# Infini-attention block: attention results kept channels-by-tokens, regrouped by DMAs, with the memory read-out transposed instead

## The chip, the cores and the metric

The kernel is one program on one core of a Trainium2 chip. The metric is the device time of one execution in microseconds (us). The core has five engines that run side by side, each working through its own queue in order: TensorE (PE, matmuls and transposes; its weight loads are listed as PEld), VectorE (DVE), ScalarE (ACT), GpSimd (POOL) and SyncE (SP), which issues nearly all DMAs of this kernel. A DMA is issued in order by its queue, moves on 16 shared DMA engines, and has landed some microseconds later.

## The reference

A transformer block over 2048 tokens of 512 channels (32 heads of 16), with the tokens in four segments of 512. The attention half, per segment `s`:

```python
logits = jnp.einsum("bhqd,bhkd->bhqk", qs, ks) * scale + mask
p = _softmax(logits, axis=-1)
a_dot = jnp.einsum("bhqk,bhkd->bhqd", p, vs)
pq = phi(qs)
num = jnp.einsum("bhld,bhde->bhle", pq, M)
den = jnp.einsum("bhld,bhd->bhl", pq, z)[..., None] + 1e-6
a_mem = num / den
o = g * a_mem + (1.0 - g) * a_dot
...
M = M + jnp.einsum("bhld,bhle->bhde", pk, vs)
z = z + jnp.einsum("bhld->bhd", pk)
```

The `o` of all heads is multiplied by `wo`, scaled and added to the input; a layer norm and a bilinear gated feed-forward layer follow. Everything is float32; large products are made from two-part splits (a high part `H` and a remainder `L`).

## The kernel before, in words

**Units.** The 32 heads stand in four groups (`g`) of eight; a group's channels fill 128 partitions. A unit `u` is four heads of one segment: `u = 8 s + 2 g + j`, 32 units in all, two to each segment and group (`ug = u // 2`).

**The loop** (lines 998 to 1039) runs over `v` from -2 to 32 with five slots each, and its order is written out by hand: PE's instructions are chained one behind the other (`pe`, line 73), DVE's too (`Chain`); those of ACT, POOL and SP are ordered by the framework's planner. In slot `i` of turn `v` come score products for a later unit (`q_step`, PE, then a masked row maximum on DVE), the products that are exponentiated for unit `v` (`k_step`, PE, ACT `pt`, then a causal select on POOL), and in slot 1 the products with the values for unit `v-1` (`av_step`, 32 matmuls into `tb`). `av_step` leaves in `tsb` (ACT, line 353), for each of the four heads `j`, 16 rows of numerators at partition `32 j` and one row of row sums at `32 j + 16`, each row 512 tokens long.

Before a unit's `k_step` its row maxima go through DVE (`n_split`), a PE transpose (`ntp`), a DVE copy `nt` and two 4 KB DMAs into `qst` (`n_step`, line 304, emitted in slot 2 of the turn before). In slot 1 stand the two 384 KB loads of a unit three turns ahead (line 259), which read what the projections wrote (`kd`, `qd`, lines 715 and 718).

**`t_step`** (lines 355 to 380, slot 4) turns `tsb` to tokens-by-channels: four PE transposes into `tr`, a DVE reciprocal of the row sums, a DVE multiplication into `orow`. For the second unit of a group POOL adds the memory part (`memb`, loaded in line 364, for `s > 0`) and SP writes 256 KB to `od` (line 379).

**Filler.** Projections, memory, and after them the output projection are generators (`fill_a`, `fill_b`) whose steps `fill` (line 929) puts between the slots. Four of the five slots add 0.25 x 5.5 = 1.375 credits; a step takes its yielded credits off, and filling goes on while credit is positive. A yielded `False` ends the filling of that slot whatever the credit.

**Memory** (`a_mem`, line 768): for `s > 0` it reads the running memory with `phi(q)` (`up`), divides (DVE `den`, POOL `mem`, lines 792 to 794) and writes 256 KB to `memd` (line 795).

**Output projection**: `wo_load` brings `od` back, `wo_op` (line 425) transposes it again, 128 x 128 blocks, four for each group, into a PSUM bank `op`, and splits that into `oH` (ACT) and `oL` (DVE); `wo_row` multiplies by `wo`; `wo_mm` runs 4 x 4 such rows. `osegs` counts the segments whose `od` is complete.

After the loop the feed-forward layer runs on PE: `product` (line 1100), woven with the preparation of weights (`prep`, line 384), then `acc`.

## Time and profile before

| what | us |
|---|---|
| median of 3 runs | 889.91 |
| lowest and highest run | 889.39, 892.38 |
| the profiled execution | 892.53 |
| its span, first to last instruction | 890.8 |
| PE busy / DVE busy | 848.3 / 660.8 |
| ACT busy / POOL busy | 471.0 / 417.9 |

The profile is of one execution. Its span is the time between the first and the last instruction; 1.7 us of the execution lie around it. Busy time is a union over an engine's instructions. The ends of matmuls are modelled, and neighbouring matmuls overlap, so the start-to-start distance of two of them says more of PE's pace than their durations do. Rows of the queue of SP show how long it took to issue a DMA, and "landing" is the time from issue until the data was there.

### The profile page before, as it was taken

To read this page: it belongs to the slowest core of one execution; us is meant where nothing else is said; L and a number is where in the kernel's file an instruction comes from. 1 tells how busy PE (TensorE), PEld (TensorE's weight loads), DVE (VectorE), ACT (ScalarE), POOL (GpSimd) and SP (SyncE) were. 2 spreads that over 40 slices of the span, in tenths; PEclk is the share of its full clock that TensorE was granted. 3 is DMA by queue.
4 is the path that set the end of the run, shared out by engine and by line. 5 is a ranking of instruction groups with operands and counts; after the bars stand their busy time and mean duration, and the time that the engine had idled before them with its cause. 6 is when DMAs were issued, how large, how long until landed. Compare 5 with 4: busy or idle time off the path is not lost.

```text
span 890.8 us, 14534 instructions
## 1 busy us (share of the span) xinstructions
PE 848.3 (95%) x4951; PEld 598.1 (67%) x4952; DVE 660.8 (74%) x1756; ACT 471.0 (53%) x730; POOL 417.9 (47%) x564
## 2 busy tenths in 40 slices
PE   8988999999999999999899898999999999999998
PEld 5755666665665556565556466878878888887886
DVE  8588877897788987678788649798884856666532
ACT  3756867777677775577444654333262622333321
POOL 4544545566546574466623423887500746560000
PEclk9998999999999999999899999999999999999999
DMA  7673543746446543657861453444402341222032
GB/s 237 216 229 114 185 122 104 240 155 199 139 125 201 163 140 123 184 164 225 257 214 61 131 164 105 144 143 123 167 26 97 93 140 48 71 54 92 0 116 95
DMA packets 103515, 124.85 MB, mean 140 GB/s; under 512 B 11984, under 2 KB 71376, under 8 KB 103440
## 3 DMA queue, kind: packets, MB, share of 16 engines
q1 hardware_dynamic: 103296, 123.90, 45.3%
q8 instruction: 39, 0.64, 0.3%
q14 instruction: 36, 0.29, 0.1%
q10 hardware_dynamic: 144, 0.02, 0.0%
HBM read 80.17 MB, written 43.45 MB: 139 GB/s over the span
## 4 chain that ended last, share of the span: by engine, by line
PE 65%; DVE 16%; DMA 8%; ACT 5%; POOL 3%; issue 2%; SPq 1%; DVEq 0%; POOLq 0%; ACTq 0%
PE g L86 20%; PE acc L86 14%; PE tb L86 6%; DVE q L40 6%; PE k L86 5%; PE q L86 5%; PE vps L86 4%; PE kps L86 2%; PE qps L86 2%; PE wops L86 2%; ACT pt L324 2%; DMA qd<-q 2%; DMA qst<-qd 1%; PE up L86 1%; DVE nm L40 1%
## 5 line engine op out<-in xcount | busy, mean ns | idle before, releaser
L40 DVE CUSTOM_DVE_ANT_0 q<-q,cmask 128x384 f32<-128x384 f32 (+3 forms) x512 | 246.7, 508 | 57.9 <-PE q L86 47.8
L324 ACT ACTIVATE pt<-k 128x1024 f32<-128x1024 f32 x160 | 163.8, 1024 | 76.5 <-PE k L86 74.2
L327 POOL TENSOR_SCALAR_AFFINE_SELECT pt<-pt 128x256 f32<-128x256 f32 (+1 forms) x224 | 99.0, 455 | 175.4 <-ACT pt L324 172.0
L86 PE MATMUL q<-kst,qst 96*128 96x384 bf16 (+3 forms) x512 | 102.4, 303 | 9.2 <-DVE nm L40 6.5
L86 PE MATMUL k<-qst,kst 98*128 98x384 bf16 (+3 forms) x512 | 98.4, 305 | 8.0 <-ACT pt L324 6.3
L400 POOL TENSOR_TENSOR w<-w 128x256 f32<-128x256 f32 (+1 forms) x84 | 72.4, 872 | 60.4 <-DMA w<-in_w_up_dram 57.8
L397 POOL TENSOR_TENSOR AL<-w,AH 128x512 fp32r<-128x512 f32 (+1 forms) x42 | 59.3, 1412 | 55.4 <-ACT AH L396 54.4
L86 PE MATMUL tb<-pt,v 128*32 128x512 f32 (+3 forms) x1024 | 76.3, 438 | 0.9 <-POOL pt L327 0.9
L86 PEld LDWEIGHTS <-kst 98*128 98x128 bf16 x512 | 39.0, 99 | 50.9 <-issue 42.8
L40 DVE DVE_READ_ACCUMULATOR2_ANT nm<- 128x1 f32 x512 | 72.0, 141 | 0.0
L396 ACT ACTIVATE AH<-w 128x512 fp32r<-128x512 f32 (+2 forms) x88 | 47.3, 565 | 45.7 <-POOL w L400 22.4
L86 PEld LDWEIGHTS <-qst 96*128 96x128 bf16 x512 | 43.8, 98 | 36.2 <-issue 10.0
L1319 DVE TENSOR_TENSOR mL<-mid,mH 128x512 fp32r<-128x512 f32 (+1 forms) x44 | 32.2, 735 | 41.5 <-ACT mH L1318 40.5
L86 PE MATMUL acc<-DH,mH 128*128 128x512 f32 x144 | 57.2, 397 | 0.0
L86 PE MATMUL acc<-DH,mL 128*128 128x512 f32 x144 | 56.6, 393 | 0.2 <-DVE mL L1319 0.2
L86 PE MATMUL acc<-DL,mH 128*128 128x512 f32 x144 | 56.5, 393 | 0.0
L86 PEld LDWEIGHTS tb<-pt,v 128*32 128x32 f32 x1024 | 28.7, 110 | 40.4 <-issue 34.7
L1318 ACT ACTIVATE mH<-mid 128x512 fp32r<-128x512 f32 (+1 forms) x44 | 27.1, 626 | 51.2 <-PE acc L86 50.2
L1114 ACT ACTIVATE p<-g 128x512 f32<-128x512 f32 (+1 forms) x22 | 13.1, 597 | 69.2 <-PE g L86 69.2
L397 DVE TENSOR_TENSOR AL<-w,AH 128x512 fp32r<-128x512 f32 (+3 forms) x44 | 33.8, 772 | 18.5 <-ACT AH L396 18.5
L353 ACT ACTIVATE tsb<-tb 128x512 f32<-128x512 f32 x32 | 19.1, 596 | 38.7 <-PE tb L86 38.6
L86 PE MATMUL g<-t_0H,AH 128*128 128x512 f32 (+1 forms) x88 | 34.6, 394 | 1.1 <-DVE u L1123 1.0
(278 smaller groups left out, 2097.9 us busy)
## 6 DMA issues: line engine op xcount, KB each, us to landing
kst<-kd SPq DMA_DIRECT2D x32, 384.0 KB, 4.3
qst<-qd SPq DMA_DIRECT2D x32, 384.0 KB, 5.1
wm<-in_w_mod_dram SPq DMA_DIRECT2D x24, 256.0 KB, 5.2
kd<-k SPq DMA_DIRECT2D x16, 384.0 KB, 3.8
qd<-q SPq DMA_DIRECT2D x16, 384.0 KB, 3.2
w<-in_w_gate_dram SPq DMA_DIRECT2D x40, 128.0 KB, 2.5
w<-in_w_up_dram SPq DMA_DIRECT2D x40, 128.0 KB, 3.1
wd<-dwd SPq DMA_DIRECT2D x6, 768.0 KB, 4.6
```

The lines of the kernel that those rows point to most:

```text
L40: i = getattr(self.eng, name)(*a, **k)
L86: return pe(nc.tensor.matmul(*a, **k))
L324: lpt[0] = act.activation(pt, kp, AF.Exp, scale=0.25)
L327: sels[u, i] = nc.gpsimd.affine_select(w, w, pattern=[[0, w.shape[1]], [1, P]], compare_op=ALU.is_ge, fill=0.0, base=0, channel_multiplier=-1)
L353: act.activation(tsbs[u], tbs.pop(u), AF.Copy)
L396: pin(act.activation(hi[sl], w[sl], AF.Copy))
L397: eng.tensor_sub(lo[sl], w[sl], hi[sl].bitcast(F32))
L400: pin(ce.tensor_tensor(w[:, o, :, 0:n], w[:, x, :, 0:n], w[:, y, :, 0:n], op=op))
L1114: act.activation(r["p1"], ps, AF.Copy)
L1318: pin(act.activation(mH[0:n], md[0:n], AF.Copy))
L1319: vec.tensor_sub(mL[0:n], md[0:n], mH[0:n].bitcast(F32))
```

## The change: what it does

- `od`, `orow`, `memb` and `memd` become channels-by-tokens, 128 partitions (channels of a group) by 512 tokens.
- `t_step` moves from slot 4 to slot 2 and issues eight DMAs instead of transposing: four spread a row of 512 row sums over 64 partitions x 8 (`rds`, 2 KB each), four copy 16 numerator rows to their place in `orow` (32 KB each). `r_step` (slot 4 of even turns) takes one DVE reciprocal for both units of a group and writes it to DRAM (`rdd`, 16 KB); `rb_step` (slot 1 of the next turn) reads it back with each row repeated for 16 partitions (256 KB); `o_step` (slot 3) multiplies on POOL, adds the memory part on POOL and writes `od`. The last group keeps the old way.
- `a_mem` transposes the memory read-out (four PE transposes into `mT`, an ACT copy `mTs`) before it writes `memd`, for 11 of the 12 groups with memory.
- `wo_op` no longer transposes, except for the last group: `oH` and, in place, `oL` come straight from the loaded tile. Its steps yield 0 instead of 0.45; for segment 0 `paced` turns each into `False`; those of segments 1 and 2 are woven into `wo_mm` of the segment before.
- The wait for `osegs` moves behind `wo_mm(0)`. After the loop, the first feed-forward block takes its weight preparation in other places. Tile tags and buffer counts follow.

```diff
--- before.py
+++ after.py
@@ -1,5 +1,5 @@
 from contextlib import ExitStack
-from itertools import chain
+from itertools import chain, islice
 
 import concourse.bass as bass
 import concourse.tile as tile
@@ -133,7 +133,8 @@
     qd = [[dram.tile([6, P, L], BF, name=f"qd{s}_{g}") for g in range(NG)] for s in range(NSEG)]
     kd = [[dram.tile([6, P, L], BF, name=f"kd{s}_{g}") for g in range(NG)] for s in range(NSEG)]
     memd = [[dram.tile([P, 4 * HG * DH], F32, name=f"memd{s}_{g}") for g in range(NG)] for s in range(NSEG)]
-    od = [dram.tile([4, P, D], F32, name=f"od{s}") for s in range(NSEG)]
+    od = [dram.tile([NG, P, L], F32, name=f"od{s}") for s in range(NSEG)]
+    rdd = [dram.tile([HG, L], F32, name=f"rdd{ug}") for ug in range(NSEG * NG - 1)]
     x1d = [[dram.tile([P, D], F32, name=f"x1d{s}_{t}") for t in range(4)] for s in range(NSEG)]
 
     def rows(s, t):
@@ -205,7 +206,7 @@
         yield from ln_rows(pool, xt, s, pfx)
         hH, hL = [], []
         for d in range(KT):
-            h = pool.tile([P, L], F32, tag="hf" if kept_h is None else "orl", name=f"{pfx}hf{s}_{d}", bufs=hb[2])
+            h = pool.tile([P, L], F32, tag="hf", name=f"{pfx}hf{s}_{d}", bufs=hb[2])
             ln_col(bank(f"{pfx}tp{s}_{d}"), h, xt, d, sc, sh, A)
             hi = hpool.tile([P, L], F32R, tag=hb[0].format(d), name=f"{pfx}hH{s}_{d}", bufs=hb[1])
             lo = hpool.tile([P, L], F32R, tag=hb[0].format(4 + d), name=f"{pfx}hL{s}_{d}", bufs=hb[1])
@@ -251,7 +252,7 @@
     vec.memset(cmask, 0.0)
     nc.gpsimd.affine_select(cmask, cmask, pattern=[[-1, L]], compare_op=ALU.is_ge,
                             fill=NEG, base=L - P, channel_multiplier=1)
-    orows, mems, ptiles, sels, tbs, tsbs = {}, {}, {}, {}, {}, {}
+    orows, rds, mems, ptiles, sels, tbs, tsbs = {}, {}, {}, {}, {}, {}, {}
 
     def load(u):
         s, g, j = u // 8, u // 2 % 4, u % 2
@@ -352,32 +353,62 @@
             tsbs[u] = ap.tile([P, L], F32, tag="tsb", name=f"tsb{u}", bufs=2)
             act.activation(tsbs[u], tbs.pop(u), AF.Copy)
 
+    def last(ug):
+
+        return ug == NSEG * NG - 1
+
+    def m_load(ug):
+
+        if ug >= NG:
+            mems[ug] = ap.tile([P, L], F32, tag="memb", name=f"memb{ug}", bufs=2)
+            nc.sync.dma_start(mems[ug], memd[ug // NG][ug % NG])
+
     def t_step(u):
 
-        s, g, jq = u // 8, u // 2 % 4, u % 2
-        ug = u // 2
+        jq, ug = u % 2, u // 2
         h0 = jq * HQ
         if jq == 0:
-            orows[ug] = wpool.tile([P, 4, HG, DH], F32, tag="orow", name=f"orow{ug}", bufs=2)
-            if s > 0:
-                mems[ug] = ap.tile([P, 4, HG, DH], F32, tag="memb", name=f"memb{ug}", bufs=2)
-                nc.sync.dma_start(mems[ug].rearrange("p t h e -> p (t h e)"), memd[s][g])
-        orow = orows[ug]
+            orows[ug] = wpool.tile([P, L], F32, tag="orow", name=f"orow{ug}", bufs=2)
         tsb = tsbs.pop(u)
-        tr = pst([P, 4, 4, 32], "sm", f"tr{u}", F32)
-        for t in range(4):
-            TP(tr[:, t].rearrange("p a b -> p (a b)"), tsb[:, t * P:(t + 1) * P], ident)
-        rd = ap.tile([P, 4, 4], F32, tag="rd", name=f"rd{u}", bufs=2)
-        vec.reciprocal(rd, tr[:, :, :, DH])
-        vec.tensor_mul(orow[:, :, h0:h0 + 4, :], tr[:, :, :, 0:DH],
-                             rd.unsqueeze(3).to_broadcast([P, 4, 4, DH]))
+        if last(ug):
+            orow = orows[ug].rearrange("p (t h e) -> p t h e", h=HG, e=DH)
+            tr = pst([P, 4, 4, 32], "sm", f"tr{u}", F32)
+            for t in range(4):
+                TP(tr[:, t].rearrange("p a b -> p (a b)"), tsb[:, t * P:(t + 1) * P], ident)
+            rd = ap.tile([P, 4, 4], F32, tag="rl4", name=f"rl4_{u}", bufs=1)
+            vec.reciprocal(rd, tr[:, :, :, DH])
+            vec.tensor_mul(orow[:, :, h0:h0 + 4, :], tr[:, :, :, 0:DH], rd.unsqueeze(3).to_broadcast([P, 4, 4, DH]))
+            if jq == 1:
+                nc.gpsimd.tensor_add(orows[ug], orows[ug], mems.pop(ug))
+            return
         if jq == 0:
-            return
+            rds[ug] = ap.tile([64, HG, 8], F32, tag="rd", name=f"rd{ug}", bufs=1)
+        for j in range(HQ):
+            nc.sync.dma_start(rds[ug][:, h0 + j], tsb[32 * j + DH:32 * j + DH + 1].rearrange("a (p k) -> a p k", k=8))
+        for j in range(HQ):
+            nc.sync.dma_start(orows[ug][(h0 + j) * DH:(h0 + j + 1) * DH], tsb[32 * j:32 * j + DH])
+
+    def r_step(ug):
+
+        rd = rds.pop(ug)
+        vec.reciprocal(rd, rd)
+        nc.sync.dma_start(rdd[ug].rearrange("h (p k) -> p h k", k=8), rd)
+
+    def rb_step(ug):
+
+        rds[ug] = ap.tile([P, L], F32, tag="rb", name=f"rb{ug}", bufs=1)
+        nc.sync.dma_start(rds[ug], rdd[ug].unsqueeze(1).to_broadcast([HG, DH, L]))
+
+    def o_step(ug):
+
+        s, g = ug // NG, ug % NG
+        o = orows.pop(ug)
+        nc.gpsimd.tensor_mul(o, o, rds.pop(ug))
         if s > 0:
-            nc.gpsimd.tensor_add(orow, orow, mems.pop(ug))
-        if ug < NSEG * NG - 1:
-            nc.sync.dma_start(od[s].rearrange("t p c -> p t c")[:, :, g * P:(g + 1) * P],
-                              orow.rearrange("p t h e -> p t (h e)"))
+            nc.gpsimd.tensor_add(o, o, mems.pop(ug))
+        nc.sync.dma_start(od[s][g], o)
+        if g == NG - 1:
+            osegs[0] += 1
 
     wt = {}
 
@@ -415,30 +446,40 @@
 
     def wo_load(s, pool):
         rw = []
-        for t in range(4):
-            a = pool.tile([P, D], F32, tag="orl", name=f"orl{s}_{t}", bufs=4)
-            n = D - P if s == NSEG - 1 else D
-            pin(nc.sync.dma_start(a[:, 0:n], od[s][t][:, 0:n]))
+        for g in range(NG - 1 if s == NSEG - 1 else NG):
+            a = pool.tile([P, L], F32, tag="orl", name=f"orl{s}_{g}", bufs=4)
+            pin(nc.sync.dma_start(a, od[s][g]))
             rw.append(a)
         return rw
 
     def wo_op(s, pb, rw, us, gs=range(NG)):
 
         for g in gs:
-            op = bank(f"op{s}_{g}")
-            for t in range(4):
-                a = rw[t][:, g * P:(g + 1) * P]
-                if s == NSEG - 1 and g == NG - 1:
-                    a = orows[NSEG * NG - 1][:, t].rearrange("p h e -> p (h e)")
-                TP(op[:, t * P:(t + 1) * P], a, ident)
-            oH = pb.tile([P, L], F32R, tag="oH", name=f"oH{s}_{g}", bufs=6)
-            oL = pb.tile([P, L], F32R, tag="oL", name=f"oL{s}_{g}", bufs=6)
-            act.activation(oH, op, AF.Copy)
+            oH = pb.tile([P, L], F32R, tag="oH", name=f"oH{s}_{g}", bufs=8)
+            if s == NSEG - 1 and g == NG - 1:
+                a = bank(f"op{s}_{g}")
+                for t in range(4):
+                    TP(a[:, t * P:(t + 1) * P], orows[NSEG * NG - 1][:, t * P:(t + 1) * P], ident)
+                oL = pb.tile([P, L], F32R, tag="oH", name=f"oL{s}_{g}", bufs=8)
+            else:
+                a = rw[g]
+                oL = a.bitcast(F32R)
+            act.activation(oH, a, AF.Copy)
             us.append((oH, oL))
-            yield 0.45
-            pin(vec.tensor_sub(oL, op, oH.bitcast(F32)))
-            if g % 2 == 1:
-                yield False
+            yield 0.0
+            pin(vec.tensor_sub(oL, a, oH.bitcast(F32)))
+            yield 0.0
+
+    def both(a, b):
+        while True:
+            x, y = next(a, None), next(b, None)
+            if x is None and y is None:
+                return
+            yield 0.0
+
+    def paced(a):
+        for _ in a:
+            yield False
 
     def xr_load(s, pb):
         xrs = []
@@ -792,7 +833,8 @@
             pin(vec.tensor_scalar_add(den, ups[:, :, :, DH], 1e-6))
             vec.reciprocal(den, den)
             nc.gpsimd.tensor_mul(mem, ups[:, :, :, 0:DH], den.unsqueeze(3).to_broadcast([P, 4, HG, DH]))
-            nc.sync.dma_start(memd[s][g], mem.rearrange("p t h e -> p (t h e)"))
+            if last(s * NG + g):
+                nc.sync.dma_start(memd[s][g], mem.rearrange("p t h e -> p (t h e)"))
         if s < NSEG - 1:
             mz = pst((P, HG, VS), "sm", f"mz{s}_{g}")
             for t in range(4):
@@ -805,6 +847,16 @@
                 vec.tensor_mul(mt, mz, hmg[:, g])
                 nc.gpsimd.tensor_add(MZ[g], MZ[g], mt)
             yield 0.9
+        elif not last(s * NG + g):
+            yield 0.0
+        if s > 0 and not last(s * NG + g):
+            mT = pst((P, L), "sm", f"mT{s}_{g}")
+            for t in range(4):
+                TP(mT[:, t * P:(t + 1) * P], mem[:, t].rearrange("p h e -> p (h e)"), ident)
+            mTs = pa.tile([P, L], F32, tag="mTs", name=f"mTs{s}_{g}", bufs=1)
+            act.activation(mTs, mT, AF.Copy)
+            nc.sync.dma_start(memd[s][g], mTs)
+            yield 0.5
         done.add((s, g, 0))
 
     def a_mod(i, a):
@@ -906,16 +958,15 @@
         pr = prep(0, "0_0", bc, 1, pb, 1)
         next(pr)
         us = [[], [], []]
-        yield from weave(wo_op(0, pb, B["orl"], us[0]), ob, (0, 1, 2, 3))
+        yield from paced(both(wo_op(0, pb, B["orl"], us[0]), ob))
+        yield from weave(wo_mm(0, us[0], pb), both(pr, wo_op(1, pb, o1, us[1])), (1, 3, 4, 6, 7, 9, 10, 12, 13))
         while osegs[0] <= 2:
             yield None
         o2 = wo_load(2, wpool)
-        yield from weave(wo_mm(0, us[0], pb), pr, (3, 6, 9, 12))
-        yield from wo_op(1, pb, o1, us[1])
         lg = lnC(0, pb, bc, pb, "x1", 4)
-        yield from weave(wo_mm(1, us[1], pb), lg, (1, 5, 6, 7, 8, 9, 11, 12, 13, 14))
+        lr = islice(lg, 10)
+        yield from weave(wo_mm(1, us[1], pb), both(lr, wo_op(2, pb, o2, us[2])), (1, 5, 6, 7, 8, 9, 11, 12, 13, 14))
         B["nxt"] = yield from lg
-        yield from wo_op(2, pb, o2, us[2])
         B["orl_free"] = True
         lg = lnC(1, pb, bc, pb, "x1", 4)
         yield from weave(wo_mm(2, us[2], pb), lg, (0, 1, 2, 3, 4, 5, 6, 7, 8, 9))
@@ -1011,7 +1062,7 @@
                     av_step(v - 1, kb)
             if v == NQ and slot == 0:
                 assert B["orl_free"]
-                o3 = wo_load(3, wpool)
+                o3 = wo_load(3, B["pb"])
                 xr3 = xr_load(3, B["pb"])
             if v == NQ and slot == 2:
                 btag[:] = ["ms", "lq0", "ms", "lq1"]
@@ -1023,9 +1074,19 @@
             if prev and slot == 4:
                 if (v - 1) % 2 == 0 and v > 8:
                     until((v - 1) // 8, (v - 1) // 2 % 4, 0)
+                if v % 2 == 1:
+                    m_load((v - 1) // 2)
+                if last((v - 1) // 2):
+                    t_step(v - 1)
+                elif v % 2 == 0:
+                    r_step((v - 2) // 2)
+            if slot == 2 and prev and not last((v - 1) // 2):
                 t_step(v - 1)
-                if (v - 1) % 8 == 7:
-                    osegs[0] += 1
+            if v > 1 and v % 2 == 1:
+                if slot == 1:
+                    rb_step((v - 3) // 2)
+                if slot == 3:
+                    o_step((v - 3) // 2)
             if slot == 2 and prev and (v - 1) % 8 == 7:
                 vfree[0] = (v - 1) // 8 + 2
             fill(share[slot], slot < 4)
@@ -1238,7 +1299,7 @@
             next(sd, None)
             for j in ((5, 6, 3, 7) if q == i == 0 else (6, 5, 2, 7, 3)):
                 product(q, i, j)
-                for _ in range(2 if i == 0 else 1):
+                for _ in range(1 if i else 0 if j == 5 else 3):
                     next(g, None)
                 if 1 < i < 9 and j in (5, 7, 3):
                     next(side, None)
```

## The prediction

> **What bounds the kernel now.** I read the page first, then the stretches of the span, the waits, the groups of instructions and one unit's timeline.
>
> ```profile
> PE 848.3 (95%) x4951; PEld 598.1 (67%) x4952; DVE 660.8 (74%) x1756; ACT 471.0 (53%) x730; POOL 417.9 (47%) x564
> PE 65%; DVE 16%; DMA 8%; ACT 5%; POOL 3%; issue 2%; SPq 1%; DVEq 0%; POOLq 0%; ACTq 0%
> L353 ACT ACTIVATE tsb<-tb x32: 585/597/603, 76.2 to 522.8; 128x512 f32<-128x512 f32 x32
> 100.00:400.00 300.00, 289.91 (x2101) 182.07 (x2100) 243.31 (x866) 210.69 (x308) 168.12 (x251) 1.00 0.53 160
> 424.00:428.00 4.00, 2.31 (x16) 1.58 (x16) 3.14 (x8) 2.45 (x5) 3.78 (x3) 1.00 0.95 295
> 428.00:435.00 7.00, 6.21 (x16) 4.79 (x15) 4.20 (x12) 2.17 (x3) 4.58 (x6) 0.51 1.06 356
> 435.00:531.00 96.00, 88.22 (x629) 54.77 (x628) 67.28 (x214) 50.68 (x68) 31.54 (x62) 0.98 0.45 142
> DVE q L40 <- PE q L86: 31.6, 50, 2.0
> ```
>
> The first row is the page's busy time, the second its chain of work. The third places the loop: 32 units from 76.2 to 522.8 us, so one takes 446.6 / 31 = 14.4 us. The windows give, for each stretch, length, busy time of PE, PEld, DVE, ACT and POOL, granted clock, DMA share and GB/s. Between 100 and 400 us PE is busy 97%, DVE 81%, ACT 70%, POOL 56%; the last row (waits in that window) shows DVE sitting idle for PE for 31.6 us. So PE sets the loop's pace, with DVE close behind, and a saving counts where both become shorter. After 424 us it is looser, with one bad spot (the clock at 0.51), which the change rebuilds.
>
> **The change, part by part: PE.**
>
> ```profile
> L89 PE MATMUL tr<-ident,tsb 128*128 128x128 f32 x128 | 19.8, 277 | 0.1
> L89 PE MATMUL op<-ident,orl 128*128 128x128 f32 x60 | 9.0, 282 | 4.0 <-DVE oL L40 4.0
> L89 PE MATMUL mp<-ident,phk 128*128 128x128 f32 x48 | 7.5, 279 | 0.0
> 339.83 0.60 PE L89 MATMUL tr<-ident,tsb 128*128 128x128 f32 x4
> 340.19 0.48 PE L86 MATMUL vps<-wvH,ahH 128*128 128x512 f32 x1
> ```
>
> Four transposes hold PE for 340.19 - 339.83 = 0.36 us where nothing stalls. Removed: 30 of 32 `t_step`s, 30 x 0.36 = 10.8; 15 of 16 `wo_op` groups, 15 x 0.36 = 5.4. Added: 11 `mT`, for which `mp` is the same form, 11 x 0.36 = 4.0. Net **-12.2 us of PE**. By busy time it is more: 120/128 x 19.8 + 9.0 - 44/48 x 7.5 = 20.7. I take 12.2, since start-to-start is what the next matmul waits for; 20.7 bounds the gain.
>
> **DVE, ACT, POOL.**
>
> ```profile
> L40 DVE RECIPROCAL rd<-tr 128x16 f32<-128x16 f32 x32 | 8.0, 250 | 0.9 <-PE tr L89 0.9
> L40 DVE TENSOR_TENSOR orow<-tr,rd 128x256 f32<-128x256 f32 x32 | 13.6, 424 | 1.3
> L40 DVE RECIPROCAL den<-den 128x32 f32<-128x32 f32 x12 | 4.2, 353 | 0.4
> L779 ACT ACTIVATE pkr<-mp 128x512 f32<-128x512 f32 x12 | 7.1, 594 | 4.5 <-PE mp L89 4.5
> L377 POOL TENSOR_TENSOR orow<-orow,memb 128x512 f32<-128x512 f32 x12 | 15.7, 1307 | 14.3 <-DVE orow L40 14.3
> ```
>
> DVE loses 30 x (0.250 + 0.424) = 20.2 us and gains 15 reciprocals of 64 elements per partition. From 16 to 32 elements the reciprocal grew by 0.10, so 64 take about 0.353 + 0.21 = 0.56 (bounds 0.35 and 0.71, twice the longest row): 8.4. Net **-11.8 us**. The `oL` subtractions stay. As PE and DVE both drop by about 12, the loop should shorten by that, whichever of them ends a slot last. ACT gains 11 copies like `pkr`, 6.5 us at 53% busy; POOL gains 15 multiplications of the size of the `orow` addition, 15 x 1.31 = 19.6 us at 47%. I cost both at nothing: POOL's selects of a unit are due only in slot 1 of the next turn. Without that cover it is 26 us.
>
> **SP and the DMAs.**
>
> ```profile
> 302.00 2.36 PE L86 MATMUL tb<-pt,v 128*32 128x512 f32 x32
> 303.72 1.62 SPq L715 DMA_DIRECT2D kd<-k  x2
> 304.43 0.60 ACT L353 ACTIVATE tsb<-tb 128x512 f32<-128x512 f32 x1 [0.74 <-PE tb L86]
> 308.36 1.15 SPq L304 DMA_DIRECT2D qst<-nt  x2
> 312.57 0.25 DVE L40 RECIPROCAL rd<-tr 128x16 f32<-128x16 f32 x1
> 314.39 0.60 PE L86 MATMUL k<-qst,kst 98*128 98x512 bf16 x2
> L304 SPq DMA_DIRECT2D qst<-nt x64: 508/515/863, 53.5 to 502.0; - x64
> DMA to landing us min/median/max: 1.6/1.7/6.6
> L259 SPq DMA_DIRECT2D kst<-kd x32: 310/328/467, 29.7 to 459.3; - x32
> SPq L304 <- DVE nt L40: 83.3, 24, 7.8
> DMA to landing us min/median/max: 2.6/5.3/6.9
> DMA to landing us min/median/max: 2.4/3.9/6.7
> ```
>
> The first six rows are one unit's timeline; then come the queue's row and landings of `nt`, the queue's row of `kst`, a wait of SP, and the landings of `memb` and of `od`. Each unit now issues eight DMAs: four of row sums, nearest to `nt` (one row to many places), 0.515 us, and four of whole rows, nearest to `kst`, 0.328: 3.4 us, with gaps some 3.8; 120 + 120 issues in the loop, and three more per group (`rdd`, `rb`, `od`; `od` was there). SP has room: it stood 83.3 us at `nt`'s DMAs waiting for DVE. `tsb` is ready at 305.03, so the eight run to 308.8, or, if `kd`'s 1.62 us come first, to 310.5; the two of `nt`, at 308.36 before, then go out until 311.6 at worst and land at 313.3, before PE's `k` needs them at 314.39. So the median unit is covered by about 1 us; a landing of 6.6 instead of 1.7 isn't. I take **+2 us** over the loop; the ends are 0 and, if every unit is 1 us late, +30. Queued behind `nt` on SP are the loads for three turns ahead; behind PE's `k` all of PE.
>
> The reciprocal would wait for the row sums: `tsb` at 3.0 us after the start of `tb`, four issues 2.1, landing 1.7 to 6.6: 6.8 to 11.7, against 312.57 - 302.00 = 10.6. In the usual case it is hidden; at the far end DVE stands 1.1 us, 15 times, 17 us. What depends on it: DVE's next `q` reductions, and by them PE's `q`. Then `rdd` must land (taken like `od`, 3.9), then `rb` (like `memb`, 5.3): 10.6 + 0.5 + 3.9 + 5.3 = 20.3 after `tb`, which is 5.9 into the next turn, about where slot 3 puts POOL's multiplication. POOL may stand for 1 or 2 us there, with selects behind it that have until the next slot 1.
>
> **The bad spot and the paced steps.**
>
> ```profile
> 414.54 2.36 PE L86 MATMUL tb<-pt,v 128*32 128x512 f32 x32
> 426.35 0.66 PE L89 MATMUL op<-ident,orl 128*128 128x128 f32 x4 [1.64 <-DVE oL L40]
> 429.42 0.63 PE L86 MATMUL wops<-woH,oL 128*128 128x512 f32 x1
> 429.85 0.63 PE L86 MATMUL wops<-woL,oH 128*128 128x512 f32 x1
> 436.14 2.36 PE L86 MATMUL tb<-pt,v 128*32 128x512 f32 x32
> ```
>
> One unit took 436.14 - 414.54 = 21.6 us instead of 14.4, as `wo_op(0)` transposed, split and waited in a row (PE stood 1.64 us for `oL`), after which the clock fell to 0.51 and matmuls came 0.43 apart. In the changed kernel `wo_op(0)` has no PE work, but its eight steps each end a slot's filling. I added the credits by hand: four slots in five give 1.375, so about 10 credits pile up while PE has no filler for 1.6 turns, and then one slot releases nearly all 16 rows of `wo_mm(0)`: 16 x 3 x 0.215 (half of 0.43) = 10.3 us of PE with little beside it. So some 7 us of the bad spot go, and about as much comes back in two quiet turns and a burst, whose first rows may run at half clock (3.4 us more if all 6.9 us are slow). I take **0**, from -7 to +7.
>
> The clock fell after 424 to 428 us, where PE was busy 2.31 of 4 us and its longest idle was 1.64 us. The Trainium skill ("TensorE: Matmul & The Clock Gate", section "HAM oscillation — how this bites in real kernels") gives as the rule that PE must not idle for more than about 3.4 us; the trace disagrees, and by the rule the quiet turns would cost nothing for the clock, while by the row up to 3.4 us.
>
> **After the loop** nothing sizeable changes: three `wo_op` groups of the last segment lose their transposes (counted above), and the weight steps move by one product. The sum: -12.2 + 2 + 0 = -10.2 us. The profiled execution took 892.53 (span 890.8), 2.6 over the median of the runs; I take the difference off the median, 889.9 - 10.2, and forecast **880 us**.
>
> **The rivals.**
>
> *Late `nt` (slower).* Eight issues ahead of `nt` eat the 1 us of cover, because the transfers share the engines with loads and land later than 1.7. It decides once PE's `k` waits in most units; at 1 us in 30 units: 889.9 - 12.2 + 30 = 908. For it: in-order SP, landings up to 6.6, the DMA share of 0.53. Against: SP waits 83.3 us for `nt` now, and the new issues fall just where it does.
>
> *Transfers in a row (slower still).* If small transfers cost their 1.7 us one after another, eight take 13.6, and `nt` lands at 305.03 + 13.6 + 1.7 = 320.3, 5.9 us late: 30 x 5.9 - 12 gives 1055. Against: two `nt` DMAs go out 0.57 apart and both land in 1.7 as a median. The Trainium skill ("DMA: Bandwidth & Descriptors", section "Rules for kernel authors") speaks for it, as it says that transfers under 64 KB are mostly overhead and should be joined; all eight here are smaller. The trace shows that overhead as a latency, not a turn.
>
> *Given back.* The loop gains 12, but the quiet turns and the burst cost their 7 with 3.4 for the clock: 889.9 - 12.2 + 2 + 10.4 = 890, no change.
>
> *More.* PE's gain is that of busy time, 20.7, and the 7 us of the bad spot go half: 889.9 - 20.7 - 3.5 + 2 = 868.
>
> *It doesn't do what it says.* If DMA landings or selects, not PE and DVE, ended the slots, nothing would come of it: 890. PE's 97% speaks against.
>
> **How the numbers follow.** Forecast (873 to 886): 0.46. More (860 to 873): 0.15. Given back or nothing (886 to 893): 0.13, of which 0.02 lie below 887 and 0.01 above 892.6. Late `nt`, or the regrouping late for DVE (17 us) or POOL: 0.24, half of it between 893 and 900. In a row: 0.02. What a measurement of this kernel can tell from no change is about 0.3%, 2.7 us: faster than 887.2 has 0.46 + 0.15 + 0.02 = 0.63, within it 0.10, slower than 892.6 0.27. The range of 8 in 10 is 866 to 899; the likeliest case's own is 873 to 886.
>
> **What would show it.** Right: units between 100 and 400 us some 0.4 us shorter (14.0 for 14.4), PE still above 95% there; `tr` at 8 and `op` at 4 transposes, `mT` at 44; DVE 12 us less busy; waits of PE's `k` for `nt` below 5 us in all; queue rows of the new DMAs between 0.33 and 0.52. Wrong: PE's `k` waiting for `nt`, DVE's reciprocal for its row sums or POOL's multiplication for `rb` by more than 10 us in all, or a stretch after 400 us longer than before.

## The result: 4% slower, and the profile after

| | median of 4 runs (3 where said), us | lowest, highest | profiled execution | its span | granted clock |
|---|---|---|---|---|---|
| before, on the same chip | 890.6 | | | | |
| before, the 3 runs above | 889.9 | 889.4, 892.4 | 892.5 | 890.8 | 0.987 |
| after | 931.2 | 923.2, 934.3 | 930.4 | 928.3 | 0.967 |

The ratio is 1.044, with a 95% interval of 1.0372 to 1.0509. The forecast was 880 us, the range 866 to 899: wrong in sign, and outside the range. One execution of a kernel below (grouped, with the transposition at no credit) took 1369 us at a granted clock of 0.56 and is left out of its median.

The page of the changed kernel, its busy times and the engines of its chain of work:

```profile
PE 850.1 (92%) x4816; PEld 593.0 (64%) x4816; DVE 653.8 (70%) x1711; ACT 478.3 (52%) x741; POOL 434.2 (47%) x579
PE 62%; DVE 12%; DMA 10%; ACT 5%; POOL 4%; issue 3%; SPq 3%; DVEq 0%; POOLq 0%; ACTq 0%
```

PE executes 135 instructions fewer and is still busy 1.8 us longer, in a span 37.5 us longer. Its share fell from 95% to 92%; in the chain the DMAs rose from 8% to 10% and SP's queue from 1% to 3%. Two windows after, then the second of them before (length, busy time of PE, PEld, DVE, ACT and POOL, granted clock, DMA share, GB/s):

```profile
100.00:400.00 300.00, 273.24 (x1939) 170.12 (x1938) 223.66 (x800) 204.18 (x297) 166.33 (x244) 0.98 0.59 166
414.00:545.00 131.00, 107.73 (x691) 62.68 (x688) 85.76 (x286) 70.64 (x99) 61.18 (x90) 0.90 0.56 167
```

```profile
414.00:545.00 131.00, 117.94 (x786) 75.91 (x785) 95.63 (x279) 69.35 (x98) 52.26 (x85) 0.96 0.51 160
```

Between 100 and 400 us PE is down from 97% to 91%, and no other engine is fuller (the rows before stand in the prediction): everything waits more. Where the time went is read from the starts of the values' products `tb`, one group of 32 for each unit. Timeline rows of PE, before and then after; the first row of each begins unit 1, the second unit 23, the third unit 29:

```profile
91.71 1.07 PE L86 MATMUL tb<-pt,v 128*32 128x512 f32 x8
400.86 1.39 PE L86 MATMUL tb<-pt,v 128*32 128x512 f32 x12
495.05 1.66 PE L86 MATMUL tb<-pt,v 128*32 128x512 f32 x8
```

```profile
93.27 1.07 PE L86 MATMUL tb<-pt,v 128*32 128x512 f32 x8
419.10 1.38 PE L86 MATMUL tb<-pt,v 128*32 128x512 f32 x11
529.04 1.39 PE L86 MATMUL tb<-pt,v 128*32 128x512 f32 x12
```

| stretch | before | after | difference |
|---|---|---|---|
| to the start of unit 1 | 91.7 | 93.3 | +1.6 |
| units 1 to 22 | 309.1 | 325.8 | +16.7 |
| units 23 to 28 | 94.2 | 109.9 | +15.7 |
| from unit 29 to the end of the span | 395.8 | 399.3 | +3.5 |

The stretches don't hold the same filler. In units 23 to 28 stand 24 products of the query projection (`qps`, 6.8 us of PE) after the change and 6 (1.9 us) before; in units 1 to 22 it is 120 and 138. So some 5 of the 15.7 us were moved there, and units 1 to 22 lost more than 16.7.

What PE and its weight loads waited for between 74 and 545 us, after (in all, times, longest):

```profile
PE k L86 <- DMA qst<-nt: 13.1, 8, 3.1
PE mT L89 <- POOL mem L835: 11.3, 5, 4.9
PEld L86 <- DMA qst<-nt: 17.7, 11, 3.4
PEld mT L89 <- POOL mem L835: 15.8, 8, 5.3
```

All eight stops of PE's first row are among the eleven of the weight loads, a few hundredths of a microsecond later, and the rows for `mT` overlap in the same way: the two rows of a wait are largely the same stops and don't add. Before, the first wait was 1.7 us once (2.1 on the weight loads), and the second didn't exist. The queue rows of the regrouping DMAs and their landings (issue min/median/max in ns; landing in us):

```profile
L387 SPq DMA_DIRECT2D rd<-tsb x120: 463/590/1476, 79.0 to 533.9; - x120
DMA to landing us min/median/max: 1.8/2.9/6.4
```

```profile
L389 SPq DMA_DIRECT2D orow<-tsb x120: 507/587/1567, 81.5 to 536.5; - x120
DMA to landing us min/median/max: 1.9/2.0/3.2
```

Eight cost 8 x 0.59 = 4.7 us of SP in a unit of 14, where the prediction had 3.4. Unit 16, whose rows before stand in the prediction, shows what that does (timeline after: start, length, engine, what; in brackets the idle time before):

```profile
314.41 2.36 PE L86 MATMUL tb<-pt,v 128*32 128x512 f32 x32
314.74 0.98 SPq L759 DMA_DIRECT2D qd<-q  x2
316.84 0.60 ACT L354 ACTIVATE tsb<-tb 128x512 f32<-128x512 f32 x1 [1.70 <-PE tb L86]
319.53 0.21 DVE L40 COPY nt<-ntp 32x128 bf16<-32x128 bf16 x1 [0.56 <-PE ntp L89]
320.36 0.32 SPq L260 DMA_DIRECT2D qst<-qd  x1
320.73 2.45 SPq L387 DMA_DIRECT2D rd<-tsb  x4
323.22 2.49 SPq L389 DMA_DIRECT2D orow<-tsb  x4
325.81 1.16 SPq L305 DMA_DIRECT2D qst<-nt  x2
```

`tsb` is ready at 317.44, but SP works in order and stands 4.5 us at the load of `qst` until what it reads, `qd`, has landed. Then the eight go out, and `nt`, copied at 319.74, leaves at 325.81, 11.4 us after the unit's start where it was 6.4 before. In units 2 to 25 the first of the two left at 8.1 to 13.0 us, before at 5.6 to 7.4. Even issues that the edit didn't touch took longer on SP: as a median 0.58 us for `nt` (0.515 before) and 0.41 for the load of `kst` (0.33). SP, which had stood 83.3 us for `nt` at these DMAs, stands there for DVE 13 us in all; for the most part DVE's result now stands in line for SP.

### The profile page after: what moved, and what is told of

It is laid out like the page before. It is cut to its first block, busy times and chain, and to the rows that moved or that the text cites. A ratio compares the mean times of both kernels' runs of the same rounds, so it can differ in the third digit from the quotient of the medians.

```text
span 928.3 us, 14709 instructions
## 1 busy us (share of the span) xinstructions
PE 850.1 (92%) x4816; PEld 593.0 (64%) x4816; DVE 653.8 (70%) x1711; ACT 478.3 (52%) x741; POOL 434.2 (47%) x579
## 4 chain that ended last, share of the span: by engine, by line
PE 62%; DVE 12%; DMA 10%; ACT 5%; POOL 4%; issue 3%; SPq 3%; DVEq 0%; POOLq 0%; ACTq 0%
PE g L86 20%; PE acc L86 13%; PE tb L86 5%; PE k L86 5%; DVE q L40 4%; PE q L86 4%; PE wops L86 3%; PE kps L86 3%; DMA qd<-q 3%; PE vps L86 3%; DMA rb<-rdd 2%; ACT pt L325 2%; PE qps L86 2%; DMA qst<-qd 1%; DMA qst<-nt 1%
## 5 line engine op out<-in xcount | busy, mean ns | idle before, releaser
L86 PE MATMUL k<-qst,kst 98*128 98x384 bf16 (+3 forms) x512 | 100.9, 311 | 24.9 <-DMA qst<-nt 13.1
L86 PE MATMUL q<-kst,qst 96*128 96x384 bf16 (+3 forms) x512 | 106.0, 313 | 13.1 <-DVE nm L40 10.1
L428 POOL TENSOR_TENSOR AL<-w,AH 128x512 fp32r<-128x512 f32 (+1 forms) x42 | 56.7, 1351 | 61.1 <-ACT AH L427 60.9
L86 PE MATMUL tb<-pt,v 128*32 128x512 f32 (+3 forms) x1024 | 79.8, 455 | 0.0
L86 PEld LDWEIGHTS <-qst 96*128 96x128 bf16 x512 | 44.9, 101 | 43.3 <-issue 16.7
L428 DVE TENSOR_TENSOR AL<-w,AH 128x512 fp32r<-128x512 f32 (+3 forms) x44 | 38.3, 873 | 13.8 <-ACT AH L427 13.7
L406 POOL TENSOR_TENSOR orow<-orow,rb 128x512 f32<-128x512 f32 x15 | 19.5, 1301 | 55.9 <-DMA rb<-rdd 24.5
```

The costliest lines, as they stand in the source:

```text
L86: return pe(nc.tensor.matmul(*a, **k))
L406: nc.gpsimd.tensor_mul(o, o, rds.pop(ug))
L428: eng.tensor_sub(lo[sl], w[sl], hi[sl].bitcast(F32))
```

## The experiments

Each was timed in three rounds against the kernel before on its chip (889.9 to 891.9 us); the median and the ratio with its interval follow each.

### SP's queue

**Two DMAs for eight.** The bytes are as many, but they are other rows, so this kernel leaves out the right regrouping.

```diff
-        for j in range(HQ):
-            nc.sync.dma_start(rds[ug][:, h0 + j], tsb[32 * j + DH:32 * j + DH + 1].rearrange("a (p k) -> a p k", k=8))
-        for j in range(HQ):
-            nc.sync.dma_start(orows[ug][(h0 + j) * DH:(h0 + j + 1) * DH], tsb[32 * j:32 * j + DH])
+        nc.sync.dma_start(rds[ug][:, h0:h0 + HQ], tsb[0:64, 0:32].rearrange("p (j k) -> p j k", k=8))
+        nc.sync.dma_start(orows[ug][h0 * DH:h0 * DH + 64], tsb[0:64])
```

> The changed kernel with two DMAs per unit in place of eight: one copies 64 whole rows to the numerators' place, one spreads 64 x 32 values for the row sums; the bytes are as many, but they are the wrong rows, so the attention output is left wrong. Theory Q (SP's issue time: eight issues of 0.59 us stand ahead of the two DMAs of nt and of the projections' writes): six issues fewer, 3.5 us of SP per unit; PE's waits of k for nt (18 us with the weight loads) fall below 4, and the time falls by 15 us or more, to 916 or less. Theory M (PE waits in mT for POOL's memory division, and POOL stands before its multiplication by rb): the waits of mT stay at 20 us or more and the time falls by less than 8, to 923 or more.

920.2 us, 1.0329 [1.0281, 1.0377]. PE's waits in `mT` rose (from 11.3 to 16.0 us on its own row, from 15.8 to 19.9 on that of the weight loads), those of the weight loads for `nt` almost went (17.7 before this edit):

```profile
PEld L86 <- DMA qst<-nt: 1.8, 3, 1.3
```

The weight loads' waits fell by 15.9 at `nt` and rose by 4.1 in `mT`: 11.8 us less, and the kernel is 11 us faster, between the two theories. SP is a part of the 40 us, not all.

**`nt` first.** `t_step` moves from slot 2 to slot 4, each of its DMAs inside `pin(...)`, which ties it behind what PE has been given by then; the steps behind it follow later, the multiplication tied as well.

```diff
...
-            if slot == 2 and prev and not last((v - 1) // 2):
+            if slot == 4 and prev and not last((v - 1) // 2):
                 t_step(v - 1)
             if v > 1 and v % 2 == 1:
                 if slot == 1:
+                    r_step((v - 3) // 2)
+                if slot == 2:
                     rb_step((v - 3) // 2)
...
```

> The eight regrouping DMAs of a unit are issued in slot 4, tied behind the DMAs of nt, and what hangs on them follows later (reciprocals slot 1 and rb slot 2 of the next odd turn, multiplication slot 0 of the next even turn, tied). Same work, the same 8 issues per unit, right output. In the changed kernel the first DMA of nt went out 8.1 to 13.0 us after a unit's start in units 2 to 25, before the change 5.6 to 7.4. Theory N (the eight issues stand in front of nt, and PE's k waits for it): nt's DMA back below 7.5 us, PE's k waiting for nt below 5 us in all (30.8 on both rows in the changed kernel), time 931 - 12 to 25 = 906 to 919. Rival Q (SP has too much to issue, whatever the order): what stands behind the eight is now late, kst and qst, kd and qd, time 922 to 935.

928.4 us, 1.0418 [1.0396, 1.0441]: the rival. The first DMA of `nt` did leave earlier, at 5.6 to 10.2 us in units 2 to 25, but SP now stood 31.9 us in all at `rb` (5.2 in the changed kernel). The queue around unit 8 (starts at 191.5), where the second DMA of `nt` left latest up to unit 26:

```profile
197.49 0.66 SPq L395 DMA_DIRECT2D rdd<-rd  x1
198.24 1.97 SPq L305 DMA_DIRECT2D qst<-nt  x1
203.56 0.66 SPq L400 DMA_DIRECT2D rb<-rdd  x1
204.27 0.53 SPq L305 DMA_DIRECT2D qst<-nt  x1
```

`rb` reads what `rdd` writes; SP stands until that has landed, and the second `nt` stands behind it, 12.8 us after the unit's start. PE's waits for `nt` were 16.5 us, and 14.4 on its weight loads: about as much as without the edit (13.1 and 17.7).

**Over DRAM, read back at once**, three issues for eight, with the multiplication late (below):

> The late, tied multiplication, and the regrouping in three DMAs per unit instead of eight: the attention rows go to DRAM whole, and one DMA brings back the row sums, one the numerators. Right output. If SP's issuing (worth 11 us by the run with two DMAs) and POOL's standing (theory B, 15 to 25) are separate losses, they add: 895 to 907. If both are one loss, because SP's lateness is what makes rb late, this is as fast as the better of the two alone: 910 to 920. If the way over DRAM makes the row sums late for the reciprocal, DVE waits for rd by more than 10 us in all and it is slower than the late multiplication alone.

934.6 us, 1.0477 [1.0423, 1.0531], 6 slower than with the late multiplication alone (928.3). SP's own wait:

```profile
SPq L389 <- DMA tsd<-tsb: 65.5, 27, 4.3
```

The read stood in the queue for the landing of its own write. Fewer issues, but a stop for a landing in front of `nt` in nearly every unit.

**Over DRAM, read back a turn later**, two units together: 4 issues per group for 16. The first line stands in `t_step` (now in slot 3), `g_step` in slot 0 of the next odd turn; the reciprocal, `rb` and the multiplication follow later, the multiplication tied (by itself, below, that gave 3 us).

```diff
+        pin(nc.sync.dma_start(tsd[ug][jq * P:(jq + 1) * P], tsb))
...
+    def g_step(ug):
+        td = tsd[ug].rearrange("(h r) t -> h r t", r=32)
+        pin(nc.sync.dma_start(rds[ug], td[:, DH].rearrange("h (p k) -> p h k", k=8)))
+        pin(nc.sync.dma_start(orows[ug], td[:, 0:DH]))
```

> Four issues per group in place of sixteen: each unit's attention rows go to DRAM whole (slot 3), and in the next odd turn's slot 0 one DMA brings back the row sums of both units and one the numerators; reciprocals slot 1, rb slot 3, multiplication slot 1 of the next even turn, tied. Right output. Theory Q (SP's issue time, 7 us per unit saved of about 10): SP's waits for the landing of the rows below 15 us in all (65.5 in the run that read them back at once), PE's k waits for nt below 8 us, time 900 to 915, below the run with nt first by at least 5. Theory N alone: the same as the run with nt first, within 5.

914.8 us, 1.0237 [1.0187, 1.0288]. Its queue rows and PE's waits for `nt`:

```profile
L385 SPq DMA_DIRECT2D tsd<-tsb x30: 319/398/931, 76.3 to 519.2; - x30
L391 SPq DMA_DIRECT2D rd<-tsd x15: 637/642/673, 98.1 to 524.1; - x15
L392 SPq DMA_DIRECT2D orow<-tsd x15: 640/652/703, 101.1 to 524.8; - x15
```

```profile
PE k L86 <- DMA qst<-nt: 9.0, 4, 3.1
```

A group costs SP 2 x 0.40 + 0.64 + 0.65 = 2.1 us in place of 16 x 0.59 = 9.4, and 16 us of the 40 come back, 13 if the late multiplication's 3 are taken off. With the run before it this says that the number of issues counts, and that none of them stands for another. It isn't all PE's wait for `nt`: that fell from 13.1 to 9.0 us (17.7 to 10.8 on the weight loads), where less than 8 had been expected.

### POOL's stand

POOL stood 55.9 us in the changed kernel before the 15 multiplications by `rb` (the page's row: busy, mean ns, idle before):

```profile
L406 POOL TENSOR_TENSOR orow<-orow,rb 128x512 f32<-128x512 f32 x15 | 19.5, 1301 | 55.9 <-DMA rb<-rdd 24.5
```

Emitting it two slots later changed nothing, as the planner put it back to the same place:

> The changed kernel with POOL's multiplication by rb, the memory addition and the write of od two slots later (slot 0 of the next turn; the last but one group stays). Theory B (POOL is blocked by its wait for rb and the row sums, some 50 us idle before it, and by that delays mem, the projections' splits and the selects): POOL's wait there falls below 15 us, PE's wait of mT for mem falls by half, the time falls by 8 us or more. Rival (mem is late because of DVE and ACT, POOL's stand is harmless): the time stays within 4 us of 931.

930.4 us, 1.0433 [1.0364, 1.0502], POOL's stand as before: no test. Tied as well (`pin(nc.gpsimd.tensor_mul(o, o, rds.pop(ug)))`):

> The multiplication by the repeated reciprocals is emitted two slots later and tied to its place behind the PE work emitted before it, so that on POOL it stands behind three more selects than in the changed kernel (in the run that only emitted it later it had stayed in front of them). Same work, right output. Theory B (POOL, in order, standing 55.9 us for rb, holds up selects and the memory products, and through them PE): POOL's wait for rb below 10 us in all, PE's waits for the memory product in mT (11.3 and 15.8 us) down to below 8 together, time 931 - 15 to 25 = 906 to 916. Rival M (PE waits in mT because the chain ups, ACT, DVE, POOL is short of time itself): POOL's wait goes, the waits of mT stay above 20 and the time stays at 925 to 932.

928.3 us, 1.0389 [1.0335, 1.0442]. POOL's wait for `rb` was gone from its list altogether, PE's waits in `mT` fell only from 11.3 to 8.4 us (15.8 to 12.7 on the weight loads), those for `nt` rose (17.7 to 24.9), and the time fell by 3, within the intervals. 56 us of standing on an engine that is busy 47% cost no more than these runs can tell apart: theory B fell.

### The memory transposition

**Left out**, so that the memory's rows are added in the wrong layout:

> Leaves out the transposition of the memory read-out: the eleven mT groups (four transposes, one ACT copy each) and their steps; memory is written as it is, so its rows are added in the wrong layout. Theory M (PE's in-order wait for mem at mT is a main loss): 27 us of waits and 4 us of transposes go, time 931 - 25 to 31 = 900 to 906. Theory B (POOL's standing is the cause and mT only one place where it shows): the wait moves to other tiles that need POOL (selects before av, q and k splits), 915 to 925. Theory Q (SP's queue sets the units): at least 925.

916.2 us, 1.025 [1.0195, 1.0305]: 15 us, where the prediction had charged 11 x 0.36 = 4. That is below theory M's 25 and in the range of theory B, but the waits didn't move to what needs POOL: those of the weight loads for `nt` rose from 17.7 to 23.3 us, in place of 15.8 in `mT`. Three ways to keep it but spare PE the wait:

**Three empty steps before it:**

> The changed kernel with mT's four transposes three filler steps later, so that POOL's memory division is done when PE comes to them; nothing else is touched. Theory M: PE's waits of mT for mem (27 us with the weight loads) fall below 6, and the time falls by 12 us or more, to 919 or less. Theory Q: the time taken from mT is lost again at k behind nt; the time falls by less than 6.

929.1 us, 1.0416 [1.036, 1.0473]; waits in `mT` 11.1 us (13.4 on the weight loads), nearly as before. Empty steps don't buy time: before the next group's products the memory queue is drained (`drain`), which runs them in a row.

**The same with `nt` first and at no credit:**

> As the run with nt first, and the transposition of memory three steps of its generator later and priced at nothing in the credit. Same work, right output. Leaving the transposition out had given 15 us. If it is PE's in-order wait for the memory product that made it dear, the waits of mT for mem fall below 8 us on both rows together (27.1 in the changed kernel) and the time is 8 to 15 us below that of the run with nt first. If it is the four transposes and the copy themselves, or the credit, no more than 5 us below.

923.5 us, 1.0368 [1.0337, 1.0399], 5 below `nt` first alone, though the waits in `mT` rose (13.1 us, 16.4 on the weight loads). With the grouped way, 909.8 us, 1.0202 [1.0172, 1.0232], also 5 below, where 888 to 902 was expected; the lowest of the kernels with the whole computation up to here:

> The grouped way over DRAM with the memory transposition later and priced at nothing. Same work, right output. If the three losses (SP's queue, PE's wait in mT, the pieces after 414 us) are separate, the first two are gone: 888 to 902, and what is left above the 878 that the removed work alone would give lies after 414 us. If below 887, it beats the kernel before; if above 910, the losses were not these two.

**Put off by about a turn**: `a_mem` puts it on a list in place of the transposes, and `fill` takes it from there five fillings later:

```diff
+            pend.append([s, g, mem, 0])
...
+        if pend:
+            pend[0][3] += 1
+            if pend[0][3] > 4:
+                mt_emit()
```

> The transposition of a group's memory is put off until five fillings (about one turn) after its product has been issued on POOL, or until the next group's memory needs the buffer; its load follows three turns later, so nothing has to hurry it. All else as in the changed kernel, right output. Theory W (PE, in order, waits at mT because its steps follow the product too closely, and the drain of the memory queue before the next key and query products uses up any empty steps put in between): waits of mT for mem below 6 us on both rows together (27.1 in the changed kernel), time 931 - 10 to 15 = 916 to 921. Rival (the wait stands in for POOL's lateness by its stand at rb, 55.9 us): waits of mT stay above 12 and the time above 925.

941.1 us, 1.0561 [1.0506, 1.0617], 10 slower, where 916 to 921 was expected; on top of the grouped way:

> The grouped way over DRAM (four issues per group in place of sixteen, multiplication late and tied) with the transposition of memory put off by a turn. Right output. If SP's issues and PE's wait at mT are two losses that add: 915 (grouped alone) - 10 to 15 = 900 to 905, the waits of mT below 6 us, and units 1 to 22 together (309.2 us before the change, 325.8 after) at 300 to 306, shorter than before by what was removed from PE. If above 910, something else holds units 1 to 22.

914.2 us, 1.0247 [1.0197, 1.0297], as the grouped way alone, where 900 to 905 was expected. Waits of `mT` for `mem` are off the list in both, and the time is no better or worse. In their place PE waits, in the first of the two, most of all:

```profile
PE up L86 <- ACT mTs L818: 5.3, 5, 1.8
```

The next read-out (`up`) waits for ACT's copy of `mT`, which frees the PSUM buffer that it needs. Besides, PE stood once for 6.6 us at a transpose `ntp` of the row maxima, for DVE. So the transposition costs 15 us, but not by that one wait: taken away there, it came back elsewhere.

### After 414 us

**No pacing** (`paced` taken off):

> The changed kernel without the pacing: the eight steps of wo_op(0) no longer end the filling of their slots. Theory P (the two quiet turns and the burst cost 14 us: 43.4 us for the two units from 469.5 us, where before took 29.0): no unit over 22 us, the time falls by 8 to 14 us, to 917 to 923. Rival (the work of the burst is only moved, DVE and ACT then stand ahead of PE as in the bad spot of before): the time stays within 4 us of 931.

935.5 us, 1.0499 [1.0444, 1.0554]: the bad spot is back, and no smaller: unit 25 takes 30.0 us (`tb` at 461.28 and 491.29).

**The burst spread**, a `False` after every third row while credit is above 1.5:

> The first segment's 16 output products give back the rest of a slot after every third row, so that the credit that has piled up isn't spent in one slot. Same work, right output. Theory P (the burst in one slot costs the 14.4 us that the units 26 and 27 lose, by PE alone at half clock and all else starved): these two units together below 32 us (43.4 in the changed kernel), time 931 - 9 to 14 = 917 to 922. Rival (the products cost the same wherever they stand, as PE is full): the two units shorten, the next ones lengthen by as much, time 927 to 932.

929.1 us, 1.042 [1.0374, 1.0465]. Starts of units 26, 27 and 28 in the changed kernel (unit 29 starts at 529.04, above), and of 26 to 29 with the burst spread:

```profile
469.55 4.50 PE L86 MATMUL tb<-pt,v 128*32 128x512 f32 x32
486.73 4.50 PE L86 MATMUL tb<-pt,v 128*32 128x512 f32 x32
512.91 2.36 PE L86 MATMUL tb<-pt,v 128*32 128x512 f32 x32
```

```profile
468.61 4.49 PE L86 MATMUL tb<-pt,v 128*32 128x512 f32 x32
485.55 3.24 PE L86 MATMUL tb<-pt,v 128*32 128x512 f32 x32
504.16 2.36 PE L86 MATMUL tb<-pt,v 128*32 128x512 f32 x32
524.89 2.36 PE L86 MATMUL tb<-pt,v 128*32 128x512 f32 x32
```

Unit 27 falls from 26.2 to 18.6, unit 28 rises from 16.1 to 20.7, as the rival had it. **Idle matmuls in the quiet turns:**

> The changed kernel with eight idle matmuls (128x256, on zeros, read by nobody) in each of the eight paced steps, so that PE has about 1 us more to do in each of these fillings. Same result, 64 matmuls more. In the changed kernel the granted clock was halved for 6.8 us at 467.44 and for 13.65 us at 477.69, in and after the two quiet turns, and so for the first part of the burst. Theory C (the quiet turns let the clock fall and the burst pays for it): no half clock between 465 and 495 us or 10 us less of it, units 26 and 27 together (43.4 us) 5 to 9 us shorter, time 922 to 926. Rival (the burst is long by its own 48 products and by what stands behind it in each engine's order): units 26 and 27 shorten by under 3 us, and the idle matmuls cost what they take, 929 to 936.

929.1 us, 1.0438 [1.0391, 1.0484]. The window of the burst, in the changed kernel and then with the idle matmuls:

```profile
477.60:491.40 13.80, 10.65 (x57) 4.25 (x55) 8.14 (x31) 4.43 (x6) 9.85 (x14) 0.51 0.60 171
```

```profile
477.60:491.40 13.80, 12.33 (x86) 8.58 (x85) 9.20 (x27) 4.74 (x7) 8.92 (x14) 1.00 0.68 203
```

The clock was mended in this window (0.51 to 1.00); an earlier spell stayed, 0.69 from 461 to 472 us. The median is 2 us lower, within the intervals, and includes the idle matmuls themselves, eight times 1.04 us on PE in the quiet turns. Units 26 and 27 took 39.9 us for 43.4: 3.5 less, between theory C (5 to 9) and its rival (under 3). On the grouped kernel with the transposition at no credit it was the same:

> The fastest right kernel so far (grouped, memory transposition three steps later and priced at nothing, 910.1) with the idle matmuls in the paced steps. By theory C 902 to 906; by its rival 909 to 915. Not expected to reach the kernel before (890), as the units 1 to 22 of that run alone are 13 us longer than the removed work would make them.

908.8 us, 1.0196 [1.0157, 1.0236], against 909.8. **Half the pacing**, on the grouped kernel with the transposition put off:

> As the grouped one with the transposition put off, and the eight paced steps before the first output products end four fillings in place of eight. Right output. Theory T (a quiet turn takes as long as DVE needs, about 15 us, so each quiet turn loses PE the 5 us of filler that would have lain beside it, and the burst pays it again): one quiet turn less, 5 to 7 us below the run with eight, about 895 to 899. Rival (PE then waits for the splits oL instead, as in the run without pacing, where units 25 and 27 took 30.0 and 18.9 us): no gain, or up to 5 us slower.

915.3 us, 1.0274 [1.0221, 1.0327], against 914.2: no gain. In five edits of this stretch units 23 to 28 took 104 to 117 us (109.9 in the changed kernel).

### Both losses taken out

> The grouped way over DRAM (four issues per group in place of sixteen), and the memory transposition left out: memory is written as it is, so its rows are added in the wrong layout. If SP's queue (16 us by the grouped run) and the memory transposition (15 us by the run without it) are separate losses, they add: 931 - 31 = 900, between 896 and 904, and the waits of k for nt stay below 12 us on both rows. If both stand for one and the same loss (whatever makes PE stand lets the clock fall, and what follows is as long with one stop as with two), 908 to 915.

898.4 us, 1.0078 [1.005, 1.0107]. The two add, within the intervals: 16.4 from the grouped way, 15.0 from the transposition, 32.8 together. Starts of units 1, 23 and 29:

```profile
88.85 1.39 PE L86 MATMUL tb<-pt,v 128*32 128x512 f32 x12
396.19 1.07 PE L86 MATMUL tb<-pt,v 128*32 128x512 f32 x8
499.72 1.71 PE L86 MATMUL tb<-pt,v 128*32 128x512 f32 x16
```

Units 1 to 22 now take 307.3 us, 1.8 less than before the change; units 23 to 28 take 103.5, still 9.3 more. What is left of the 40 us stands there, and not all of the 9.3 is a loss: 111 products with `wo` stand in these units against 96 before, some 3.5 us by an estimate of 0.23 each (their distance in the rows of PE), and from unit 29 on the span is 2.3 us shorter than before. The profiled execution was 3.5 us below the median of its kernel.

## Why the prediction was wrong, step by step

**PE's gain was right in kind.** Where nothing stalls, a unit lost 0.4 us. Starts of units 3 and 4, before and after:

```profile
119.61 2.36 PE L86 MATMUL tb<-pt,v 128*32 128x512 f32 x32
132.81 1.07 PE L86 MATMUL tb<-pt,v 128*32 128x512 f32 x8
```

```profile
121.56 2.36 PE L86 MATMUL tb<-pt,v 128*32 128x512 f32 x32
134.34 1.07 PE L86 MATMUL tb<-pt,v 128*32 128x512 f32 x8
```

13.20 to 12.78. `tr`, `op` and `mT` stand at 8, 4 and 44 as forecast. But little of it reached the time: with both losses out and no `mT`, units 1 to 22 were 1.8 us shorter, where 22 x 0.36 would be 7.9; PE still waited there for `nt`, 4.5 us in all. The whole kernel of that run took 898.4 us, where the prediction's own terms without SP's 2 and the 4.0 of `mT` give 889.9 - 12.2 - 4.0 = 873.7. So the step from work taken off PE and DVE to time ("the loop should shorten by that") failed as well, by 25 us, of which the third point below names up to 9.

**"DVE −11.8"** came out at −7.0 (660.8 to 653.8). The reciprocal took 539 ns (0.56 forecast) and waited for its row sums 0.7 us in all; the rest was lost to other rows, such as the weights' `AL`, 772 ns before and 873 after.

**"+2" for SP, the step that failed first.** "SP has room: it stood 83.3 us at `nt`'s DMAs" took idle time before one instruction for room in the queue. Those were 24 stops, 3.5 us each in the mean; the eight issues took 4.7 us, and SP now stands for landings as well (`qd`, 15.4 us in all; `rdd`, 5.2). At worst, the prediction let `nt` leave at 310.5, 8.5 us after the start of its unit; in 17 of the units 2 to 25 it left later. The rival *Late `nt`* was the mechanism, priced at 1 us in each of 30 units; by the run with two DMAs and the grouped one SP's share is 11 to 16 us, in eleven stops and not in each unit. Which part of it PE pays at `nt` and which elsewhere isn't settled: the grouped run kept more than half of the waits for `nt` and gained more. *Transfers in a row* didn't come: landings stayed at 2.0 and 2.9 us as medians. The rule of the Trainium skill quoted there ("DMA: Bandwidth & Descriptors", section "Rules for kernel authors": join small transfers) gave the right advice: joined, they gave 16 us back. As the landings were short before, the gain is argued to lie in the queue's issue time; no run joined them and kept that time.

**"+11 x 0.36" for `mT`, the second.** It was priced as four transposes. It is a stop in PE's written order behind a chain of ACT, DVE and POOL, an ACT copy, a bank of PSUM and 0.5 of credit each; leaving it out was worth 15. What is queued behind a new wait was asked for SP and DVE, and not for PE, where all of PE's later work stands behind it. Which of these parts makes up the 15 isn't settled: removing the wait alone gave nothing, and pricing the credit at nothing with three empty steps gave 5, with the waits still there. In the two profiled executions (928.3 and 917.1 us) units 1 to 22 hold 5.2 of the difference and all that follows 5.6, where only two of the eleven `mT` groups stand: a part of the 15 comes from how the filler is laid out, not from the stop itself.

**"I take 0" for the bad spot, the third.** Units 23 to 28 took 15.7 more; 9.3 of that stay without the other two losses. The half of it that was right is the bad spot: unit 24 of that run takes 15.4 us, 6.2 less than before, where 7 was forecast. "As much comes back in two quiet turns and a burst" was the wrong half: units 25 and 26 take 16.1 and 27.5 us, 2.5 and 13.8 more than before, and without filler the quiet turns didn't get short. Units 24 and 25 of that run (window as above):

```profile
409.50:441.00 31.50, 22.37 (x135) 9.74 (x135) 24.08 (x80) 19.22 (x28) 17.37 (x23) 0.75 0.75 222
```

15.75 us each, with PE busy 71% and DVE 76%: no engine is full, so "as long as DVE needs", as the expectation of half the pacing has it, isn't it either. What filler PE could have run there is paid again in the burst. That fits the rows, but no edit that filled or halved the quiet turns made the kernel faster by more than the intervals. A part of it is SP's queue again. `nt` of unit 24 was copied at 415.10 us, while SP stood 4.8 us for the landing of `rdd`; behind `rb` it left at 419.38, and PE stood 4.3 us for it:

```profile
414.95 0.15 DVE L40 COPY nt<-ntp 32x128 bf16<-32x128 bf16 x1
418.16 0.62 SPq L403 DMA_DIRECT2D rb<-rdd  x1
419.38 1.21 SPq L306 DMA_DIRECT2D qst<-nt  x2
423.12 1.01 PE L86 MATMUL k<-qst,kst 98*128 98x512 bf16 x2 [4.29 <-DMA qst<-nt]
```

In the changed kernel PE's waits for `nt` in units 23 to 28 were 7.2 us, in three stops. No run took this stop out by itself, so how the 9 us divide between it, the moved filler and the burst stays open. The half clock wasn't shown to be a part, as the idle matmuls brought no more than the intervals.

**POOL "costed at nothing" was right** within 3 us; the reason given (its selects have until the next slot 1) fits, though it stood 3.7 us in each of 15 units where 1 or 2 were forecast.

## What to carry to other kernels

A queue that stands idle before one instruction isn't free: count what each unit issues on it, with the landings it must stand for, and ask by when the instruction behind must leave. An operation added to an engine whose order is fixed can cost the chain that feeds it and the place that it takes, not only its own duration, and empty steps before it don't hide that if another rule runs them in a row. Work taken off the bounding engine gives its few tenths of a microsecond only where no wait was added beside it. And stretches between two marks compare only if the same filler stands in them.

## What the runs showed of the hardware

- A DMA's issue on SP took, as a median of its pattern, 0.38 us (`kd`) to 0.67 (`rdd`) in the changed kernel; row sums over 64 partitions and 16 rows between partitions 0.59, `rb` with repeated rows 0.66, single ones up to 1.57. Whole rows to DRAM (`tsd`) took 0.40 in the grouped kernel. It isn't the pattern alone: the unchanged load of `kst` took 0.33 before and 0.41 after.
- What a halved clock cost here lies below what these runs tell apart. In the changed kernel PE was granted 0.51 for 13.8 us in the densest stretch of the loop; with that window at 1.00, and the idle matmuls' own time in it, the median was 2 us lower, within the intervals.
- The clock fell at 467.44 us, just after PE's longest idle time in that stretch, 3.1 us (3.4 on its weight loads) for `nt` until 467.04. The Trainium skill ("TensorE: Matmul & The Clock Gate", section "HAM oscillation — how this bites in real kernels") puts the limit at about 3.4 us of idle time. This fall is too near to it to tell; the one before the change, with 1.64 us as the longest idle time, came earlier than that.
